# One fused attention and ELU kernel: engine orders written out in a table, one pool of PSUM banks, and batch 0 loaded another way

## The chip, the cores and the metric

The kernel runs on one core of a Trainium2 chip. The metric is the device time of one execution in microseconds. A core has five engines with queues of their own: TensorE (PE; its weight loads are listed as PEld), VectorE (DVE), ScalarE (ACT), GpSimd (POOL) and SyncE (SP, which here only starts transfers). Each works through its own list of instructions in order and waits on semaphores for the others.

## What is computed

Attention over 8 batches and 8 heads, 576 tokens, head size 64, with 16 beacon keys and values ahead of the causal ones, and then an MLP with an ELU on the 4608 rows that come out, 512 -> 2048 -> 512.

```
k_all = concat(beacon_k, k); v_all = concat(beacon_v, v)
scores = q @ k_all.T / sqrt(D)           # causal over k, beacons always seen
a = softmax(scores)
x = (a @ v_all) as rows of 4608 x 512    # (b, s) x (h, d)
h = x @ w_in
out = where(h > 0, h, exp(min(h, 0)) - 1) @ w_out
```

Inputs and output are float32 in HBM.

## The kernel before

**Attention.** Two heads make a pair (n = 0 to 31, four to a batch). For batches 0 to 2, keys and queries of a pair are loaded together into one staging tile (`load_pair`, L308), cast to bf16 (`cast_pair`, L317) and transposed on TensorE (`do_T2`, L394, for batch 0; `do_T`, L384, for 1 and 2); DVE and ScalarE copy the result to `kT` and `qT`. For batches 3 to 7 rows of tokens are loaded (`load_tok`, L332), cast, and transposed by a DMA (`turn_tok`, L350). Scores come out transposed, keys on partitions: `do_SC` (L432) makes four units of a pair, of up to 512 columns for each head, on 64 rows of the array for each head. `do_exp` (L445) takes exp on ScalarE, `do_mask` (L452) clears what is not causal on GpSimd, `do_AV` (L460) multiplies by the values with a column of ones, and `do_norm` (L481) divides by the sums on DVE. Batches 0 and 1 go back through TensorE (`do_xT`, `do_xcopy`) to `xT`, later ones by a DMA (`turn_x`, L357).

**Values.** `load_v` (L362) loads 128 tokens of all heads at a time, each row of a head 256 bytes, from SP or ScalarE's queue; `cast_v` (L371) casts on DVE.

**MLP.** The rows are cut into eleven tiles, 128, 128, 256 and then 512 rows. For each tile sixteen steps (fewer for the small ones) of `do_mm1` (L521) write one bank; `do_e` (exp, ScalarE), `do_clamp` (GpSimd) and `do_join` (DVE) make the ELU; `do_mm2` (L556) sums quarters of the second product, `do_osb` copies it out and `do_store` stores it from SP's queue. Weights come in eight loads from GpSimd's queue, cast on the way (`load_w`, L375).

**What sets the order.** Everything is an `Op` of a `Plan` (L18 to L140) with an engine, a key (its due time), a cost, its dependences, and the buffers that it takes and gives. `Plan.run` plays this through on the host when the kernel is built and writes down each engine's order; the constants from L577 on (SHIFT, AT, PACES, TOK ...) set the keys. Where TensorE would be idle before a planned 30 us it puts in a matmul that computes nothing (`do_fill`, L271).

**PSUM.** Of eight banks, two buffers of two banks have the tag `sc` (scores, and transposes of batches 1 and 2), four of one bank the tag `ff` (the rest). Scores of units (0,1) and (2,3) of a pair are issued together (batch 0: unit 0, units 1 and 2, unit 3).

Of the kernel before, what the change touches and what calls it, by code (L numbers as in the profile page):

```python
# [10 lines left out]
FP32 = mybir.dt.float32  # L11
# [4 lines left out]
P = 128  # L16


class Op:
    def __init__(self, eng, key, dur, fn, deps=(), take=(), give=(), mode=None, lat=0.03, queue=0, parts=1):  # L20
        self.eng, self.key, self.dur, self.fn = eng, key, dur, fn
        self.deps, self.take, self.give = [d for d in deps if d is not None], take, give
        self.mode, self.lat, self.queue, self.parts = mode, lat, queue, parts
        self.left, self.after, self.rest = 0, [], parts


class Plan:
    MODE_COST = 0.1

    def __init__(self, slots, window):  # L30
        self.slots, self.window, self.ops = dict(slots), window, []

    def add(self, *args, **kw):
        op = Op(*args, **kw)
        self.ops.append(op)
        return op

    def run(self):
        for i, op in enumerate(self.ops):
            op.seq = i  # L40
            op.left = len(op.deps)
            for d in op.deps:
                d.after.append(op)
        ready = {op.eng: [] for op in self.ops}
        pending = {eng: sorted((o.key, o.seq) for o in self.ops if o.eng == eng) for eng in ready}
        done = set()
        first = dict.fromkeys(pending, 0)
        free = dict.fromkeys(pending, 0.0)
        mode, lines, turn = None, ([], [], []), 0

        def arrive(o):
            if o.eng == "DMA":
                lines[o.queue].append(o)
            else:
                heapq.heappush(ready[o.eng], (o.key, o.seq))

        for op in self.ops:
            if not op.left:
                arrive(op)
        events, order, now, n_left, tick = [], [], 0.0, len(self.ops), 0  # L60
        while n_left:
            for eng in ready:
                if free[eng] > now + 1e-9:
                    continue
                if eng == "DMA":
                    if any(lines):
                        turn = next((turn + i) % 3 for i in (1, 2, 3) if lines[(turn + i) % 3])
                        op = lines[turn][0]
                        free[eng] = now + op.dur / op.parts
                        heapq.heappush(events, (free[eng], tick, None))  # L70
                        tick += 1
                        op.rest -= 1
                        if not op.rest:
                            lines[turn].pop(0)
                            heapq.heappush(events, (free[eng] + op.lat, tick, op))
                            tick += 1
                    continue
                line = pending[eng]
                while first[eng] < len(line) and line[first[eng]][1] in done:
                    first[eng] += 1  # L80
                if first[eng] == len(line):
                    continue
                limit = line[first[eng]][0] + self.window.get(eng, 1e9)
                skipped, op = [], None
                while ready[eng]:
                    item = heapq.heappop(ready[eng])
                    o = self.ops[item[1]]
                    if item[0] > limit:
                        skipped.append(item)
                        break  # L90
                    if all(self.slots[t] >= o.take.count(t) for t in o.take):
                        op = o
                        break
                    skipped.append(item)
                for item in skipped:
                    heapq.heappush(ready[eng], item)
                if op is None:
                    if eng == "PE" and now < self.fill_until and self.slots["ff"]:
                        mode = 0
                        order.append((now, len(order), self.filler))  # L100
                        free[eng] = now + (self.cold_dur if now < self.cold_until else self.filler.dur)
                        heapq.heappush(events, (free[eng], tick, None))
                        tick += 2
                    continue
                for t in op.take:
                    self.slots[t] -= 1
                start = now
                if op.mode is not None:
                    if mode not in (None, op.mode):
                        start += self.MODE_COST  # L110
                    mode = op.mode
                done.add(op.seq)
                order.append((start, len(order), op))
                free[eng] = start + op.dur
                heapq.heappush(events, (free[eng], tick, None))
                heapq.heappush(events, (free[eng] + op.lat, tick + 1, op))
                tick += 2
            assert events, (self.slots, [(o.key, o.eng, o.left) for o in self.ops if o.seq not in done][:10])
            now = events[0][0]
            while events and events[0][0] <= now + 1e-9:  # L120
                _, _, op = heapq.heappop(events)
                if op is None:
                    continue
                n_left -= 1
                for t in op.give:
                    self.slots[t] += 1
                for o in op.after:
                    o.left -= 1
                    if not o.left:
                        arrive(o)  # L130
        self.length = now
        self.order = order
        for _, _, op in order:
            if op.fn is not None:
                op.fn()
# [3 lines left out]
def kernel(  # L139
# [30 lines left out]

    HALF = P // 2
    G = S // HALF
    assert G * HALF == S
    NKC = -(-SK // P)
# [8 lines left out]
    class Cut:  # L183
        def __init__(self, ranges, splits):
            self.ranges, self.parts, self.units, self.of_range = ranges, [], [], []
            for (lo, hi), split in zip(ranges, splits):
                part = [(jc, max(lo, first_q[jc]), hi - max(lo, first_q[jc])) for jc in range(NKC) if first_q[jc] < hi]
                self.parts.append(part)
                self.of_range.append(list(range(len(self.units), len(self.units) + len(split))))
                for chunks in split:  # L190
                    self.units.append([p for p in part if p[0] in chunks])
            self.col_of, self.width, self.unit_of = {}, [], {}
            for u, unit in enumerate(self.units):
                col = 0
                for jc, q0, w in unit:
                    self.col_of[jc, q0], self.unit_of[jc, q0] = col, u
                    col += w
                assert col <= 512
                self.width.append(col)

    CUT = Cut([(0, 240), (240, 496), (496, 576)], [[(0, 1)], [(0, 1), (2, 3)], [(0, 1, 2, 3, 4)]])

# [5 lines left out]
    def blocks_of(groups):  # L208
        lo, hi = CUT.ranges[groups[0]][0], CUT.ranges[groups[-1]][1]
        return [i for i, (q0, w, _) in enumerate(BLOCKS) if lo <= q0 < hi]  # L210
# [15 lines left out]
    NG, NET, NKQ = 18, 8, 2 * HP  # L226
    NST, NSB, NVST = 6, 3, 6
    PE_B = 3
    konst = ctx.enter_context(tc.tile_pool(name="konst", bufs=1))
    big = ctx.enter_context(tc.tile_pool(name="big", bufs=1))  # L230
    stage = ctx.enter_context(tc.tile_pool(name="stage", bufs=2))
    attn = ctx.enter_context(tc.tile_pool(name="attn", bufs=2))
    melt = ctx.enter_context(tc.tile_pool(name="melt", bufs=4))
    gpool = ctx.enter_context(tc.tile_pool(name="gpool", bufs=NG))
    opool = ctx.enter_context(tc.tile_pool(name="opool", bufs=3))

    ctx.enter_context(tc.manual_schedule())

    identb = konst.tile([P, P], BF16, name="identb")
    make_identity(nc, identb)  # L240
    identh = konst.tile([P, P], FP16, name="identh")
    make_identity(nc, identh)
    fill0 = nc.gpsimd.to_reg(0.0)

    RING = 4 * S
    xTa = big.tile([P, NCC, RING], FP16, name="xT")
    xT = [xTa[:, cc] for cc in range(NCC)]
    w_in16 = big.tile([P, NCC, DF], FP16, name="w_in16")
    w_out16 = big.tile([P, NFC, DM], FP16, name="w_out16")
# [12 lines left out]
    with tc.tile_pool(name="psum", bufs=1, space=bass.MemoryType.PSUM) as psum:  # L262
# [21 lines left out]
        def load(key, dur, fn, deps=(), take=(), issue=0.47, units=1, on="SP"):  # L284
# [3 lines left out]
            if "vst" not in take and on + str(key) != "ACT-899":  # L288
                issues["st"].append(issue)
# [588 lines left out]
```

## Time and profile before

| | us |
|---|---|
| listed runs | 355.49, 1955.26, 353.3 |
| median | 355.49 |
| span of the profiled execution, first to last instruction | 352.5 |
| TensorE busy | 343.3 |
| DVE / ScalarE / GpSimd busy | 205.8 / 194.1 / 179.4 |

The time of the profiled execution itself is not listed; the lowest listed run is 0.8 us above its span. TensorE had its full clock in all slices of the profile. A row of a timeline is start, length, engine, line, operation, what is written <- what is read, and the number of instructions merged; a bracket tells how long the engine was idle before and what ended that. Names such as L473 are lines of the kernel before.

### The profile page before, as it was taken

Reading aid. Unit: us, or ns where it says so; the run is one execution under the profiler, and the core shown is the slowest. Engines: PE = TensorE matmul, PEld = TensorE weight load, DVE = VectorE, ACT = ScalarE, POOL = GpSimd, SP = SyncE. Lnnn points to the kernel's source line nnn. Section 1 sums busy time; section 2 is a strip of 40 time slices with the busy share of each in tenths; the row PEclk is TensorE's granted clock in tenths of the full one; section 3 lists DMA queues with packets and bytes.
Section 4 is the critical chain, followed back from the end, with each engine's and each line's share of the span. In section 5 each row is a group of like instructions: output and inputs, shape, how many; then the busy total and the mean of one; then the engine's idle time right before and its main releaser. Section 6 shows DMA issues by size and latency. Waiting matters only on the chain.

```text
span 352.5 us, 8440 instructions
## 1 busy us (share of the span) xinstructions
PE 343.3 (97%) x3295; PEld 195.6 (55%) x3295; DVE 205.8 (58%) x428; ACT 194.1 (55%) x289; POOL 179.4 (51%) x353
## 2 busy tenths in 40 slices
PE   8999999999999989999999999999999999999996
PEld 5668887545555445545476664554445544444444
DVE  1478797557556567557746565764665555455322
ACT  2586887577556746684576547663477443343200
POOL 5587776556635655475475455463554333434200
PEclk9999999999999999999999999999999999999999
DMA  7999996798998979899999679767460220000112
GB/s 189 260 286 221 206 238 130 227 215 146 165 209 144 208 153 185 160 195 204 152 232 150 146 138 237 143 104 182 96 144 32 60 69 32 31 31 32 47 72 91
DMA packets 139480, 52.55 MB, mean 149 GB/s; under 512 B 127536, under 2 KB 131888, under 8 KB 139440
## 3 DMA queue, kind: packets, MB, share of 16 engines
q1 hardware_dynamic: 87472, 35.55, 46.7%
q10 hardware_dynamic: 47744, 12.26, 18.9%
q0 software_dynamic: 4224, 4.19, 7.1%
q8 instruction: 26, 0.43, 0.5%
q14 instruction: 14, 0.11, 0.1%
HBM read 37.22 MB, written 9.44 MB: 132 GB/s over the span
## 4 chain that ended last, share of the span: by engine, by line
PE 82%; DMA 7%; DVE 4%; SPq 2%; POOL 1%; issue 1%; ACT 1%; ACTq 0%; POOLq 0%; DVEq 0%
PE ops L563 32%; PE hps L529 32%; PE av L473 8%; PE sc L439 7%; DMA st<-in_k_dram 3%; PE spare L274 3%; DMA st<-in_q_dram 2%; DMA xT<-x 1%; SPq L314 1%; DMA kT<-st 1%; DVE gt L549 1%; POOL et L454 1%; DVE x L489 1%; ACT et L448 1%; POOL e L540 1%
## 5 line engine op out<-in xcount | busy, mean ns | idle before, releaser
L529 PE MATMUL hps<-xT,w_in 128*128 128x512 f16 (+2 forms) x768 | 141.4, 326 | 2.8 <-DVE gt L549 1.3
L563 PE MATMUL ops<-w_out,gt 128*128 128x512 f16 (+1 forms) x592 | 143.9, 374 | 0.0
L549 DVE SCALAR_TENSOR_TENSOR gt<-e,hps 128x512 f16<-128x512 f32 x144 | 97.6, 684 | 74.9 <-POOL e L540 74.5
L540 POOL TENSOR_SCALAR e<-e 128x512 f32<-128x512 f32 x144 | 88.1, 614 | 102.4 <-ACT e L536 100.5
L536 ACT ACTIVATE e<-hps 128x512 f32<-128x512 f32 x144 | 85.6, 600 | 94.3 <-PE hps L529 90.2
L448 ACT ACTIVATE et<-sc 128x768 f16<-128x768 f32 (+3 forms) x128 | 104.1, 863 | 31.8 <-PE sc L439 31.6
L529 PEld LDWEIGHTS <-w_in 128*128 128x128 f16 x768 | 68.0, 98 | 57.6 <-issue 3.6
L563 PEld LDWEIGHTS <-gt 128*128 128x128 f16 x592 | 54.1, 98 | 56.5 <-issue 3.0
L454 POOL TENSOR_SCALAR_AFFINE_SELECT et<-et 128x256 f16<-128x256 f16 (+2 forms) x160 | 61.5, 410 | 44.9 <-ACT et L448 40.8
L473 PEld LDWEIGHTS <-et 128*128 128x128 f16 (+1 forms) x960 | 36.1, 97 | 11.0 <-issue 2.2
L569 DVE COPY osb<-ops 128x512 f32<-128x512 f32 (+1 forms) x37 | 25.0, 675 | 26.2 <-PE ops L563 25.3
L473 PE MATMUL av<-v,et 128*128 128x65 f16 (+1 forms) x960 | 39.7, 193 | 0.3 <-DVE x L489 0.3
L439 PE MATMUL sc<-qT,kT 64*128 64x80 bf16 (+3 forms) x704 | 35.2, 228 | 0.3 <-ACT qT L428 0.2
L489 DVE TENSOR_TENSOR x<-av,rl 128x256 f16<-128x256 f32 (+2 forms) x68 | 32.1, 472 | 2.3
L439 PEld LDWEIGHTS <-kT 64*128 64x128 bf16 x704 | 20.7, 95 | 18.9 <-issue 16.8
L488 DVE RECIPROCAL rl<-av 128x4 f32<-128x4 f32 (+2 forms) x68 | 12.4, 182 | 21.4 <-PE av L473 20.3
L373 DVE CAST v<-vst 128x512 f16<-128x512 f32 (+1 forms) x40 | 21.1, 529 | 4.1 <-DMA vst<-in_v_dram 4.1
L274 PE MATMUL spare<-ones 128*128 128x256 bf16 x111 | 19.1, 304 | 1.6 <-DVE ones L816 1.3
L274 PEld LDWEIGHTS <-ones 128*128 128x128 bf16 x111 | 10.9, 109 | 6.2 <-issue 1.7
L346 DVE CAST st<-st 128x1024 bf16<-128x1024 f32 (+2 forms) x18 | 11.6, 655 | 2.8 <-DMA st<-in_k_dram 1.4
L323 POOL CAST st<-st 128x1152 bf16<-128x1152 f32 x8 | 9.1, 1142 | 5.7 <-DMA st<-in_q_dram 3.9
L346 POOL CAST st<-st 128x1024 bf16<-128x1024 f32 (+2 forms) x12 | 10.7, 892 | 2.0 <-DMA st<-in_k_dram 2.0
(35 smaller groups left out, 68.0 us busy)
## 6 DMA issues: line engine op xcount, KB each, us to landing
out_dram<-osb SPq DMA_DIRECT2D x35, 256.0 KB, 2.6
st<-in_q_dram ACTq DMA_DIRECT2D x20, 256.0 KB, 4.3
vst<-in_v_dram ACTq DMA_DIRECT2D x15, 256.0 KB, 4.1
st<-in_k_dram SPq DMA_DIRECT2D x15, 256.0 KB, 5.0
st<-in_k_dram SPq DMA_DIRECT2D x12, 288.0 KB, 7.1
st<-in_q_dram SPq DMA_DIRECT2D x11, 288.0 KB, 6.9
vst<-in_v_dram SPq DMA_DIRECT2D x9, 256.0 KB, 7.0
w_in<-in_moe_w_in_dram POOLq DMA_DIRECT2D x4, 512.0 KB, 12.7
```

The source lines that it names most:

```text
L274: nc.tensor.matmul(out=spare[:, 0:2 * P], lhsT=ones[:, 0:P], rhs=ones, start=True, stop=True)
L439: nc.tensor.matmul(out=sc[:, h, o:o + w], lhsT=kT[D * h:D * h + D, P * jc:P * jc + P], rhs=qT[D * h:D * h + D, q0:q0 + w], start=True, sto ...
L448: nc.scalar.activation(out=et[:, :, 0:w], in_=scs[n, u][:, :, 0:w], func=AFT.Exp, bias=0.0, scale=float(1.0 / (D ** 0.5)))
L454: nc.gpsimd.affine_select(out=et[:, :, c0:c0 + dw], in_=et[:, :, c0:c0 + dw], compare_op=ALU.is_ge, fill=fill0, base=q0 + NB - P * jc, pat ...
L473: nc.tensor.matmul(out=av[:, c:c + D + 1], lhsT=ets[n, CUT.unit_of[jc, at]][0:m, h, col:col + P], rhs=v16[0:m, jc, 2 * hp + h, 0:D + 1], s ...
L489: nc.vector.tensor_tensor(out=x16s[b % 2][:, blks[0]:blks[0] + nb, P * hp:P * hp + P].rearrange("q i (h d) -> q i h d", d=D), in0=av[:, :, ...
L529: nc.tensor.matmul(out=hps[:, o:o + z - a], lhsT=w_in16[:, cc, P * fc:P * fc + P], rhs=xT[cc][:, a % RING:a % RING + z - a], start=(cc == ...
L536: nc.scalar.activation(out=e, in_=hpss[tt, i], func=AFT.Exp, bias=0.0, scale=1.0)
L540: nc.gpsimd.tensor_scalar(out=e, in0=e, scalar1=1.0, scalar2=0.0, op0=ALU.min, op1=ALU.max)
L549: nc.vector.scalar_tensor_tensor(out=gt, in0=es[tt, i], scalar=1.0, in1=hpss[tt, i], op0=ALU.subtract, op1=ALU.max)
L563: nc.tensor.matmul(out=opss[tt, t4][:, cols], lhsT=gts[tt, fc][:, P * t4:P * (t4 + 1)], rhs=w_out16[:, fc, cols], start=(fc == 0), stop=(f ...
L569: nc.vector.tensor_copy(out=osb[:, slice(*cols)], in_=opss[tt, t4][:, slice(*cols)])
```

## The change

The planner is gone. The kernel lists its ops with dependences, buffers and the engines that could do each, and three tables say the rest: ORDER, the order of all ops (with -1 for a filler matmul and the bank that it writes), PICKS, which engine does an op that more than one could do (casts, copies, and SP or ScalarE for starting a load), and PLACES, which buffer each op takes. `Program.run` only plays the tables.

```diff
-        self.slots, self.window, self.ops = dict(slots), window, []
...
+    def run(self, order, picks, places, fill):
+        picks, places, used = iter(picks), iter(places), set()
+        for op in self.ops:
+            if len(op.engines) > 1:
+                op.eng = next(picks)
+        for i in order:
+            if i < 0:
+                at = int(next(places), 36)
+                fill(self.rooms["bank"][at])
+                continue
+            op = self.ops[i]
...
+            for room in op.take:
+                at = int(next(places), 36)
+                held = [("bank", at), ("bank", at + 1)] if room == "pair" else [(room, at)]
...
+                op.fn(self.engines[op.eng], *got, *op.args)
```

PSUM is eight banks in one pool. Scores and the transposes of batches 1 and 2 take an even bank and the next, all else takes one bank; every score unit is now an op of its own.

```diff
-            "sc": 2, "ff": 4, "av": 2, "ops": 1, "et": NET, "rl": 2, "e": NE, "gt": NG, "osb": 3,
...
+    pairs = [psum.tile([P, 2, 512], FP32, name=f"banks_{i}") for i in range(4)]
...
+        "bank": [pairs[i // 2][:, i % 2] for i in range(8)],
+        "pair": [pairs[i // 2] for i in range(8)],
+        "acc": [None, None],
```

Keys and queries of batch 0 are loaded, cast, transposed and copied in two parts, 256 tokens and 320, with a bank for each; scores of unit 0 need only the first part.

```diff
+    CUTS = (0, 256, S)
...
+    def do_T2(e, bank, n, half):
+        tr = trs[n, half] = bank.bitcast(BF16)
...
+        for g in range(g1):
+            e.transpose(
+                out=tr[:, P * g:P * g + P], in_=b16s[n][:, g0 + g].rearrange("p h d -> p (h d)"), identity=identb)
...
+            need = ready if b else ready[0] + (ready[1] if u else [])
```

Of batch 0's values the first 512 of 592 rows (beacons included) are loaded by three DMAs from GpSimd's queue, four tokens to a partition (runs of 1 KB of a head), cast to fp16 on the way, into the room of the last quarter of `w_out16`. TensorE puts them in order: for each 128 rows four matmuls of 32 rows and 512 columns with a matrix of ones and zeros (`sel`, which GpSimd makes by a memset and four selects). ScalarE or DVE copies them out. The last 80 rows, and batches 1 to 7, go the old way. The last quarter of `w_out` is loaded after that.

```diff
+    def do_sel(e):
+        e.memset(sel, 0.0)
+        for c in range(P // 32):
+            e.affine_select(
+                out=sel, in_=sel, compare_op=ALU.not_equal, fill=1.0, base=P * c,
+                pattern=[[-1, VG], [1, P]], channel_multiplier=-VG)
...
+    def load_vq(e, b, part):
+        r0, r1 = [(0, NB // VG), (NB // VG, 64), (64, P)][part]
+        src = beacon_v[b] if part == 0 else v[b, :, VG * r0 - NB:VG * r1 - NB, :]
+        e.dma_start(out=vq[r0:r1], in_=src.rearrange("h (p g) d -> p h (g d)", g=VG))
...
+    def do_P(e, bank0, bank1, b, half):
+        for g in range(VG):
+            for c, bank in ((2 * half, bank0), (2 * half + 1, bank1)):
+                vps[b, c] = bank
+                rows = slice(32 * c, 32 * c + 32)
+                e.matmul(
+                    out=bank, lhsT=sel[rows, g, :], rhs=vq[rows, :, D * g:D * g + D],
+                    start=(g == 0), stop=(g == VG - 1), skip_group_check=True)
```

The memsets of the beacon tiles and of the ends of the exp tiles move from GpSimd to DVE, casts of values and of rows of tokens may be GpSimd's or DVE's for each op, and copies DVE's or ScalarE's. Tiles, matmul shapes, exps, masks and the MLP's steps are as before, and so is what goes through DMA transposes. Counted in the orders that the two programs issue:

| | before | after |
|---|---|---|
| filler matmuls | 111 | 57 |
| matmuls that put values in order | 0 | 16 |
| runs of score matmuls on TensorE, all / behind the first MLP matmul | 68 / 56 | 59 / 48 |
| DMAs started by SP / ScalarE / GpSimd | 191 / 56 / 8 | 181 / 69 / 11 |

On TensorE the changed order starts with 21 fillers, the first half of pair 1, 10 fillers, the first half of pair 2, scores of pair 1, then values in order. Ahead of the first MLP matmul stand all scores, value matmuls and transposes back of batch 0 and the transposes of pairs 6 and 4; before, two of the value matmul ops and four of the transposes back stood behind it. The last stores are issued as the first half of the last block, the whole block before it, the second half.

More of the change, by code (lines that the diff above doesn't have):

```diff
@@ L1 @@
-import heapq
-from functools import partial
 from contextlib import ExitStack
@@ L16 @@
 P = 128
-class Op:
[L20 to L30, printed above, removed]
-        self.slots, self.window, self.ops = dict(slots), window, []
[L33 to L55, printed above, removed]
-        for op in self.ops:
[L58 to L133, printed above, removed]
-            if op.fn is not None:
-                op.fn()
@@ L173 @@
     assert G * HALF == S
+    CUTS = (0, 256, S)
+    GS = [(z - a) // HALF for a, z in zip(CUTS, CUTS[1:])]
+    VG = 4
     NKC = -(-SK // P)
@@ L208, in blocks_of @@
     def blocks_of(groups):
[L209 removed]
+        lo, hi = RANGES[groups[0]][0], RANGES[groups[-1]][1]
         return [i for i, (q0, w, _) in enumerate(BLOCKS) if lo <= q0 < hi]
@@ new lines, with copy, fill @@
+    plan = Program({"P": nc.tensor, "V": nc.vector, "A": nc.scalar, "G": nc.gpsimd, "S": nc.sync, "-": None}, rooms)
+    add = plan.add
+    f32s, b16s, vsts, bks = {}, {}, {}, {}
+    trs, scs, ets, avs, xts, vps = {}, {}, {}, {}, {}, {}
+    hpss, es, gts, opss, osbs = {}, {}, {}, {}, {}
+    def copy(e, out, in_):
+        if e is nc.scalar:
+            e.activation(out=out, in_=in_, func=AFT.Copy)
+        else:
+            e.tensor_copy(out=out, in_=in_)
+    def fill(bank):
+        nc.tensor.matmul(out=bank[:, 0:2 * P], lhsT=ones[:, 0:P], rhs=ones, start=True, stop=True)
@@ new lines, in cast_pair, with cast_pair2, do_T @@
+    def cast_pair(e, sb, n, half):
+        b16s[n] = sb
+        cast_pair2(e, n, half)
+    def cast_pair2(e, n, half):
+        if half is None:
+            dst, src, g = b16s[n], f32s[n], G
+        else:
+            g = GS[half]
+            g0 = CUTS[half] // HALF
+            dst, src = b16s[n][:, g0:g0 + g], part_of(f32s[n], half)
+        copy(e, dst.rearrange("p g h d -> p h g d"), src.rearrange("p h (g d) -> p h g d", g=g))
+    def do_T(e, pair, n):
+        b, hp = divmod(n, HP)
+        tr = trs[n] = pair.rearrange("p a b -> p (a b)").bitcast(BF16)
+        for g in range(G):
+            e.transpose(out=tr[:, P * g:P * g + P], in_=b16s[n][:, g].rearrange("p h d -> p (h d)"), identity=identb)
+        e.transpose(out=tr[:, P * G:P * G + P], in_=bk16s[b % 2][:, P * hp:P * hp + P], identity=identb)
@@ new lines, in turn_x, with do_xT @@
+    def turn_x(e, b, blk):
+        q0, rows, _ = BLOCKS[blk]
+        e.dma_start_transpose(
+            out=xTa[:, :, b * S % RING + q0:b * S % RING + q0 + rows], in_=x16s[b % 2][0:rows, blk, :])
+    def do_xT(e, bank, n, groups):
+        b, hp = divmod(n, HP)
+        xt = xts[n, groups[0]] = bank.bitcast(FP16)
+        lo = RANGES[groups[0]][0]
+        for blk in blocks_of(groups):
+            q0, rows, _ = BLOCKS[blk]
+            e.transpose(
+                out=xt[:, q0 - lo:q0 - lo + rows], in_=x16s[b % 2][0:rows, blk, P * hp:P * hp + P],
+                identity=identh[0:rows, 0:rows])
@@ new lines, in add_tok @@
+    def add_tok(b):
+        turned[b] = []
+        for is_k in (True, False):
+            for c in range(0, NKC, 2):
+                m = min(2, NKC - c)
+                st = add("SA", load_tok, b, is_k, c, take=["st"])
+                got = [st] + ([add("SA", load_tok2, b, is_k, c + 1, deps=[st])] if m == 2 else [])
+                cast = add("GV", cast_tok, b, is_k, c, m, deps=got, take=["sb"], give=[(st, 0)])
+                for j in range(m):
+                    before = [o for hp in range(HP) for o in last_SC.get((b - 2) * HP + hp, [])]
+                    turned[b].append(add("S", turn_tok, b, is_k, c + j, deps=[cast] + before))
+                add("-", None, deps=turned[b][-m:], give=[(cast, 0)])
@@ new lines @@
+    gts_in = {}
+    make_identity(nc, identb)
+    make_identity(nc, identh)
+    nc.vector.memset(ones, 1.0)
+    for t in kTa:
+        nc.vector.memset(t[:, :, SK:SKP], 0.0)
+    for t in bk16s:
+        nc.vector.memset(t, 0.0)
+    for et in rooms["et"]:
+        nc.vector.memset(et[:, :, WIDTH[-1]:WIDTH[-1] + P - BLOCKS[-1][1]], 0.0)
+    for t in v16s:
+        nc.vector.memset(t[:, :, :, D:VW], 1.0)
+    sel_done = add("G", do_sel)
+    for b in range(B):
+        add_batch(b)
+    for f4 in range(4):
+        add_w(0, f4)
+        add_w(1, f4)
@@ L851 @@
+    for p in range(NTT):
+        add_tile(p)
+    for b, t in turns:
+        t.deps += readers.get(b - RING // S, [])
+    plan.run(ORDER, PICKS, PLACES, fill)
 _INS = ['q', 'k', 'v', 'beacon_k', 'beacon_v', 'moe_w_in', 'moe_w_out']
```

955 lines of the change are left out of this document (409 added, 546 removed), and 71 rows, old and new, of the table ORDER.

## The prediction

> **What bounds the kernel now.** I read the page first, then the stage table, then the timelines of TensorE, ScalarE and GpSimd over the first 36 us, the groups by form, the DMA view of two stretches, and the waits.
>
> ```profile
> span 352.5 us, 8440 instructions
> PE 343.3 (97%) x3295; PEld 195.6 (55%) x3295; DVE 205.8 (58%) x428; ACT 194.1 (55%) x289; POOL 179.4 (51%) x353
> ...
> PE 82%; DMA 7%; DVE 4%; SPq 2%; POOL 1%; issue 1%; ACT 1%; ACTq 0%; POOLq 0%; DVEq 0%
> ```
>
> TensorE is busy for 97% of the span and holds 82% of the chain that ended last. A sum over the run hides stages, so the stage table is cut at the first matmul of the MLP (31.9 us), and at the last matmul. Its columns are the stretch, its length, then busy time and count of each engine, the granted clock, the DMA share and GB/s.
>
> ```profile
> 0.00:31.90 31.90, 28.91 (x364) 20.91 (x365) 16.36 (x54) 17.58 (x26) 22.10 (x50) 1.00 1.08 238
> 31.90:60.00 28.10, 27.82 (x458) 23.44 (x458) 22.95 (x54) 22.34 (x35) 19.72 (x38) 1.00 1.10 210
> 60.00:150.00 90.00, 88.06 (x897) 46.94 (x896) 55.25 (x118) 55.51 (x80) 47.85 (x97) 1.00 0.93 178
> 150.00:349.40 199.40, 198.51 (x1582) 104.35 (x1582) 110.82 (x204) 98.64 (x150) 89.69 (x171) 1.00 0.54 114
> 349.40:352.60 3.20, 0.00 (x0) 0.00 (x0) 0.41 (x1) 0.00 (x0) 0.00 (x0) 1.00 0.27 99
> ```
>
> From 31.9 to 349.4 us TensorE is idle for 0.28 + 1.94 + 0.89 = 3.1 us. No order of the engines can win more than that there, except by making TensorE's own work shorter. The first stretch is different. The same view for the filler matmuls alone:
>
> ```profile
> 0.00:31.90 31.90, 19.05 (x111) 10.86 (x111) 1.00 1.08 238
> ```
>
> 111 of the 364 matmuls there compute nothing; they stand where TensorE would wait. So the gain to look for is in the first 32 us, a smaller one in TensorE's own work, and the 3.2 us of the last store stay.
>
> **The start.** The MLP's first matmul needs all four head pairs of batch 0 through exp, so ScalarE's queue sets the time. Rows of the timelines, one of the stage table, then of the groups by form (count | busy us, mean ns):
>
> ```profile
> 1.83 0.98 POOL L820 MEMSET bk<- 128x512 bf16 x2
> ```
> ```profile
> 5.80 1.14 POOL L323 CAST st<-st 128x1152 bf16<-128x1152 f32 x1 [2.03 <-DMA st<-in_q_dram]
> ```
> ```profile
> 9.76 0.78 ACT L448 ACTIVATE et<-sc 128x736 f16<-128x736 f32 x1 [1.17 <-PE sc L439]
> ```
> ```profile
> 9.76:31.90 22.14, 20.55 (x311) 15.21 (x310) 14.70 (x46) 15.52 (x23) 16.97 (x30) 1.00 1.20 256
> ```
> ```profile
> L448 ACT ACTIVATE et<-sc 128x768 f16<-128x768 f32 (+3 forms) x128 | 104.1, 863 | 31.8 <-PE sc L439 31.6
> ```
> ```profile
> L536 ACT ACTIVATE e<-hps 128x512 f32<-128x512 f32 x144 | 85.6, 600 | 94.3 <-PE hps L529 90.2 <-DVE x L489 1.8 <-DVE st L346 1.2
> ...
> L454 POOL TENSOR_SCALAR_AFFINE_SELECT et<-et 128x256 f16<-128x256 f16 x96 | 39.6, 428 | 21.3 <-ACT et L448 20.0 <-PE hps L529 0.5
> ...
> L373 DVE CAST v<-vst 128x512 f16<-128x512 f32 x32 | 17.3, 540 | 4.1 <-DMA vst<-in_v_dram 4.1
> ...
> L454 POOL TENSOR_SCALAR_AFFINE_SELECT et<-et 128x160 f16<-128x160 f16 x32 | 11.6, 364 | 0.7 <-ACT et L448 0.6
> ...
> L428 ACT ACTIVATE qT<-tr 128x576 bf16<-128x576 bf16 x8 | 5.2, 649 | 5.9 <-DVE kT L423 4.7 <-PE av L473 1.2
> ...
> L380 POOL DMA_DIRECT2D w_out<-in_moe_w_out_dram x4 | 3.7, 920 | 0.0
> ```
>
> First exp. Batch 0's keys and queries now come as two loads each, the first 256 of 576 tokens. The old first cast began at 5.80 when 288 KB of queries landed; 128 KB should land between a proportional 3 us and 5.8, I take 5.5. The cast is now DVE's (540 ns for 512 elements), so pair 1 is transposed at 6.1. Its first scores stand behind pair 2's transposes on TensorE, whose cast is on GpSimd behind two value loads (920 ns each), a memset of 512 elements (0.5 us, as each of the two at 1.83) and four selects of 512 elements. From 428 ns at 256 and 364 ns at 160 elements a select grows by 0.67 ns per element, so 0.6 us each. The other memsets leave GpSimd for DVE, which is idle then. GpSimd: 1.8 + 1.8 + 0.5 + 2.4 = 6.5, plus a cast of 0.6 (half of the 1.14): 7.1; half a pair's transposes, scores and handovers, about 1.1 us: first exp at 8.2 instead of 9.76.
>
> ScalarE's queue from there to the last exp of batch 0: 16 exps at 104.1 / 128 = 0.81 (13.0), two copies of ordered values like the 600 ns ACTIVATE (1.2), two query copies of at most 649 ns (1.3): 15.5 us. If ScalarE never waited it would end at 23.7. Before, from 9.76 to 31.9, ScalarE (the fourth engine of the row) was busy 15.5 of 22.1 us, so it waited 6.6. Waits of 0 to 6.6 us give 23.7 to 30.3. I take 3, near the middle: transfers still come late, but each half needs only half of them. Then 26.7; plus the last values matmuls, reciprocal and multiply, transpose and copy, about 1.5 us: first MLP matmul at 28.2 (25.2 to 31.8) instead of 31.9. **Term 1: -3.7 us** (-6.7 to -0.1).
>
> In the changed order every value matmul and transpose back of batch 0 and two transposes of batch 1 stand ahead of that matmul. Before, two sets of ten value matmuls, five transposes back and the ten transposes of a pair of batch 1 stood behind it; that matmul's row and their rates, by starts:
>
> ```profile
> 31.91 1.05 PE L529 MATMUL hps<-xT,w_in 128*128 128x128 f16 x16 [0.54 <-DVE xT L510]
> 32.80 0.28 PE L499 MATMUL xt<-identh,x 128*128 128x128 f16 x2
> 32.91 0.47 PE L473 MATMUL av<-v,et 128*128 128x65 f16 x10
> 33.23 0.20 PE L499 MATMUL xt<-identh,x 80*128 80x80 f16 x1
> ```
>
> Ten value matmuls take 0.32 us (32.91 to 33.23), two transposes 0.11 (32.80 to 32.91). So 0.64 + 15 x 0.055 = 1.5. **Term 2: -1.5 us.** The 16 matmuls that put the values in order (512 columns, at most 0.22 us each by the rows below: 1.8 to 3.5 us) come before it too, in place of 54 fillers that are gone (57 are left), so nothing for them, unless ScalarE waits for their copies; that is in the 0 to 6.6.
>
> **TensorE's own work.** Scores run on 64 rows of the array, all else on 128. The switch shows in the starts:
>
> ```profile
> 139.57 0.52 PE L439 MATMUL sc<-qT,kT 64*128 64x256 bf16 x14
> 140.02 0.35 PE L473 MATMUL av<-v,et 128*128 128x65 f16 x6
> 140.21 1.89 PE L563 MATMUL ops<-w_out,gt 128*128 128x512 f16 x8
> 142.03 0.55 PE L439 MATMUL sc<-qT,kT 64*128 64x240 bf16 x8
> 142.52 1.90 PE L563 MATMUL ops<-w_out,gt 128*128 128x512 f16 x8
> 144.26 0.35 PE L473 MATMUL av<-v,et 128*128 128x65 f16 x6
> ```
>
> Eight matmuls take 1.74 us before values (142.52 to 144.26) and 1.82 before scores (140.21 to 142.03): 0.08 to enter. Units 2 and 3 are 784 columns, with both heads side by side 0.33 us at 512 columns in 0.218, and take 0.45 (139.57 to 140.02): 0.12 to leave. Behind the first MLP matmul the old order enters scores 56 times, the new one, which places single units and groups those of several pairs, 48 times: 8 x 0.2. **Term 3: -1.6 us.** [...]
>
> **Waits behind.** The eight banks in one pool and finer score units could remove the 3.1 us of idle time; a fixed order over five queues could add as well. I take no change: -3 to +14 (rival C). **Tail:** the second-last store is now issued right before the last and shares the engines with it: +0.2 (0 to +1, by the 3.2 us row). DVE's memsets at the start (2 us) stand before its first cast and cost nothing while data are on the way.
>
> Sum: -3.7 - 1.5 - 1.6 + 0.2 = -6.6: span 345.9. The lowest run shown, 353.3, is 0.8 over the profiled span; with that the time is **346.7**. The median shown, 355.5, is 2.2 above its own execution; against it this is -2.5%, against 353.3 -1.9%. A difference under about 2% can't be told from none here.
>
> **Rivals.** *A, better:* ScalarE never waits in the start and half of the later idle time goes: -3.0 - 1.6, time 342.1. For it: it waited 6.6 us there, and most of its idle rows end with TensorE, which had fillers in hand; against: the DMA engines are full throughout that stretch (share 1.08).
>
> *B, no gain in the start, since transfers set it.* DMA queue rows (packets, MB, share of 16 engines) of 0 to 34 us and of 300 to 345 us, where only stores run:
>
> ```profile
> q10 hardware_dynamic: 4976, 1.51, 22.6%
> ```
> ```profile
> q1 hardware_dynamic: 1032, 1.88, 11.2%
> ```
>
> In the first, 0.226 x 16 x 34 = 123 us for 4976 packets: 25 ns for 303 B, 12 B/ns. In the second, 0.112 x 16 x 45 = 81 us for 1032 packets: 78 ns for 1822 B, 23 B/ns. Values of batch 0 went in rows of 256 B, now 88% of them go in runs of 1 KB, so they cost the engines about half: 1.05 MB at 12 B/ns on 16 engines is 5.5 us, at 23 B/ns 2.9. That speaks for the change. Against it: two of their three loads now run ahead of or beside the first keys, on a third queue. [...] No row here shows GpSimd's queue in the first 20 us. As a mechanism of this kernel: 1.05 MB at the 238 GB/s of the first stretch is 4.4 us; if all of that stands in front of the keys of pairs 2, 0 and 3, it eats the 3.7 of term 1: time 350.4.
>
> *C, slower: ScalarE held at its own DMA issues.* By the order that the two programs issue, ScalarE issues 69 DMAs instead of 56, SP 181 instead of 191, GpSimd 11 instead of 8 (the three value loads). [...]
>
> ```profile
> ACT e L536 <- DVE x L489: 1.8, 1, 1.8
> ```
> ```profile
> SPq L369 <- DVE rl L488: 6.2, 2, 5.7
> ```
>
> Before, such a wait held ScalarE for 1.8 us once; on SP, where nothing else stands behind, one for a value load took 5.7. When ScalarE stops, TensorE goes on until its banks are full: eight banks are at most eight MLP steps, 4 x 0.218 each, 7 us, but four score units or fewer when scores are next, about 1 us. Three waits of 5.7 us that meet a run of scores, less 1 us each, are 14.1 us: 346.7 + 14.1 = 360.8. It decides from 6.6 us of uncovered waits on, which is the whole sum.
>
> **Chances.** Forecast 0.46 (own range 343.5 to 349.5), A 0.13, B 0.21, C 0.20. Against the median shown, 2% less is 348.4, against the lowest run 346.2. So faster by over 2% takes A and four fifths of the forecast: 0.13 + 0.37 = 0.50. Within 2%: the rest of the forecast and B, 0.09 + 0.21 = 0.30. Slower by over 2%: C, 0.20. The range goes from A to B with the 3 to 5 us of the waits' bounds on top: 341.5 to 356.0; C and a little below A stay out.
>
> **What would show it.** Term 1: the first MLP matmul at 25.2 to 31.8, 57 fillers, the first exp near 8.2 and ScalarE's waits from there to its last exp of batch 0. Term 2: no transpose back of batch 0 behind that matmul. Term 3: 48 entries into scores, with the same 0.2 for each. Waits: TensorE's idle time from there to the last matmul near 3 us; over 10 with ScalarE behind a DMA issue is C. B: value matmuls or pair 0's cast waiting for their loads past 11 us. It would be wrong if TensorE's idle time grew with no DMA behind it, for instance where a bank that the table names is freed late while another is free, or if the first MLP matmul came no earlier than 31.

## The result, and the profile after

The changed kernel takes 477.62 us in the median (477.41 to 480.24, 5 runs) where the kernel before takes 353.67: ratio 1.348 (95% interval 1.340 to 1.356), 35% slower. The forecast was 346.7, its range ended at 356.0. The profiled execution took 480.24 us, its span is 478.2. Lines of the kernel after are named as in its profile. Its page:

```profile
span 478.2 us, 8360 instructions
...
PE 371.6 (78%) x3257; PEld 205.6 (43%) x3257; DVE 203.5 (43%) x429; ACT 193.6 (40%) x290; POOL 180.7 (38%) x363
...
PE 57%; DVE 13%; ACT 9%; DMA 7%; issue 5%; POOL 5%; SPq 3%; DVEq 0%; ACTq 0%; POOLq 0%
...
L550 PE MATMUL banks<-xT,w_in 128*128 128x512 f16 (+2 forms) x768 | 148.2, 345 | 45.4 <-DVE gt L568 25.5
L588 PE MATMUL banks<-w_out,gt 128*128 128x512 f16 (+1 forms) x592 | 142.3, 384 | 28.7 <-DVE gt L568 12.0
```

TensorE fell from 97% to 78% of the span, and no other engine took over: each is below half. The last two rows are the two products of the MLP. Together they stood idle 74 us, and what ended the idle time is ahead of all DVE's join, an engine that is busy 43% of the time. The stage table, cut again at the first MLP matmul and the last matmul; the first fence is before in one stretch, the second after:

```profile
31.91:349.40 317.49, 314.40 (x2931) 174.73 (x2930) 189.01 (x375) 176.48 (x264) 157.25 (x304) 1.00 0.70 141
```
```profile
0.00:43.37 43.37, 30.19 (x361) 21.30 (x362) 21.09 (x75) 18.37 (x27) 22.34 (x48) 0.83 0.97 222
43.37:473.60 430.23, 341.44 (x2897) 184.28 (x2896) 181.69 (x353) 175.25 (x264) 158.31 (x315) 0.94 0.48 97
473.60:478.20 4.60, 0.00 (x0) 0.00 (x0) 0.73 (x2) 0.00 (x0) 0.00 (x0) 0.71 0.33 114
```

From these rows the 125.7 us between the two spans (478.2 less 352.5) come apart: the start +11.5 (43.37 less 31.91), TensorE's idle time behind it +85.7 (430.23 - 341.44 = 88.8, less 3.1), its busy time there +27.0, and the tail +1.4 (4.6 less 3.2). So most of it is waiting, spread over the whole run, with a lower granted clock on top. The waits, summed over the span (times, longest):

```profile
ACT e L557 <- DVE gt L568: 26.1, 18, 3.4
PE banks L550 <- DVE gt L568: 25.5, 14, 5.1
DVE gt L568 <- PE banks L550: 22.4, 7, 7.7
DVE gt L568 <- PE banks L588: 20.4, 10, 3.7
PE banks L550 <- ACT e L557: 12.4, 12, 2.9
PE banks L588 <- DVE gt L568: 12.0, 9, 2.2
PE banks L588 <- ACT e L557: 8.7, 8, 2.2
```

Some of these make no sense by the algorithm. A join (L568) needs the first product and the clamped exp, not a result of the second product (L588). In the profile of before, no join of DVE waited for a matmul of the second product and no MLP matmul of TensorE for an exp of ScalarE. One such wait in the timeline:

```profile
227.54 0.62 ACT L557 ACTIVATE e<-banks 128x512 f32<-128x512 f32 x1
...
228.21 1.89 PE L550 MATMUL banks<-xT,w_in 128*128 128x512 f16 x8 [2.86 <-ACT e L557]
```

By the PLACES table this matmul writes bank 3, and the exp that it waited 2.86 us for reads bank 2. Nothing else joins the two: banks 2 and 3 are the two halves of one declared tile, `pairs[1]`.

### The profile page after: what moved, and what is told of

Same layout as the page of the kernel before. It is cut to its first block, busy times and chain, and to the rows that moved or that the text cites. A ratio compares the mean times of both kernels' runs of the same rounds, so it can differ in the third digit from the quotient of the medians.

```text
span 478.2 us, 8360 instructions
## 1 busy us (share of the span) xinstructions
PE 371.6 (78%) x3257; PEld 205.6 (43%) x3257; DVE 203.5 (43%) x429; ACT 193.6 (40%) x290; POOL 180.7 (38%) x363
## 4 chain that ended last, share of the span: by engine, by line
PE 57%; DVE 13%; ACT 9%; DMA 7%; issue 5%; POOL 5%; SPq 3%; DVEq 0%; ACTq 0%; POOLq 0%
PE banks L588 25%; PE banks L550 22%; DVE gt L568 6%; ACT e L557 6%; PE banks L498 6%; POOL e L561 4%; DMA st<-in_q_dram 3%; DVE x L512 2%; DMA vst<-in_v_dram 2%; PE banks L468 2%; ACT et L477 2%; DMA st<-in_k_dram 2%; DVE osb L594 2%; PE banks L349 1%; DVE rl L511 1%
## 5 line engine op out<-in xcount | busy, mean ns | idle before, releaser
L550 PE MATMUL banks<-xT,w_in 128*128 128x512 f16 (+2 forms) x768 | 148.2, 345 | 45.4 <-DVE gt L568 25.5
L588 PE MATMUL banks<-w_out,gt 128*128 128x512 f16 (+1 forms) x592 | 142.3, 384 | 28.7 <-DVE gt L568 12.0
L568 DVE SCALAR_TENSOR_TENSOR gt<-e,banks 128x512 f16<-128x512 f32 x144 | 94.7, 684 | 135.0 <-POOL e L561 71.7
L557 ACT ACTIVATE e<-banks 128x512 f32<-128x512 f32 x144 | 82.6, 598 | 148.4 <-PE banks L550 93.8
L477 ACT ACTIVATE et<-banks 128x1024 f16<-128x1024 f32 (+3 forms) x128 | 104.6, 863 | 91.8 <-PE banks L468 81.2
L588 PEld LDWEIGHTS <-gt 128*128 128x128 f16 x592 | 56.7, 99 | 92.4 <-issue 39.6
L498 PE MATMUL banks<-v,et 128*128 128x65 f16 (+1 forms) x960 | 42.5, 199 | 12.6 <-ACT e L557 3.4
L594 DVE COPY osb<-banks 128x512 f32<-128x512 f32 (+1 forms) x37 | 24.8, 674 | 48.5 <-PE banks L588 37.2
L468 PE MATMUL banks<-qT,kT 64*128 64x80 bf16 (+3 forms) x704 | 36.1, 234 | 7.9 <-DVE gt L568 3.4
L512 DVE TENSOR_TENSOR x<-banks,rl 128x256 f16<-128x256 f32 (+2 forms) x68 | 32.1, 471 | 2.3
L404 DVE CAST sb<-st 128x1024 bf16<-128x1024 f32 (+2 forms) x21 | 12.6, 610 | 0.0
L294 POOL CAST sb<-st 128x512 bf16<-128x512 f32 (+2 forms) x7 | 5.5, 796 | 11.5 <-DMA st<-in_q_dram 11.3
```

What stands on the lines that cost most here:

```text
L294: e.tensor_copy(out=out, in_=in_)
L468: e.matmul(out=pair[:, h, o:o + w], lhsT=kT[D * h:D * h + D, P * jc:P * jc + P], rhs=qT[D * h:D * h + D, q0:q0 + w], start=True, stop=True ...
L477: e.activation(out=et[:, :, 0:w], in_=scs[n, u][:, :, 0:w], func=AFT.Exp, bias=0.0, scale=float(1.0 / (D ** 0.5)))
L498: e.matmul(out=av[:, c:c + D + 1], lhsT=ets[n, unit_of[jc, at]][0:m, h, col:col + P], rhs=v16s[b % 2][0:m, jc, 2 * hp + h, 0:D + 1], start ...
L512: e.tensor_tensor(out=x16s[b % 2][:, blks[0]:blks[0] + nb, P * hp:P * hp + P].rearrange("q i (h d) -> q i h d", d=D), in0=av[:, :, :, 0:D] ...
L550: e.matmul(out=bank[:, o:o + z - a], lhsT=w_in16[:, cc, P * fc:P * fc + P], rhs=xTa[:, cc, a % RING:a % RING + z - a], start=(cc == 0), st ...
```

## The theory, and the experiments

**Theory S (shared tiles).** The eight banks are declared as four tiles of two banks. By this theory the framework that sets the semaphores orders a write of a tile behind every open use of that tile, and a read behind its last write, whichever half they touch. So two ops in neighbouring banks wait for each other. In the built program of after, some 130 of TensorE's instructions and some dozens each of DVE's and ScalarE's wait for one that touched only the neighbour bank. In that of before hardly any do: there only scores and the transposes of batches 1 and 2 had tiles of two banks, and a unit or pair used both. **Rival O (order).** The written-out order, or which bank the table names, sets the waits; tiles don't matter.

**One bank per tile.** So that each instruction stays within a tile, each exp of scores is cut in two, one per head, and the copies out of the transposes of batches 1 and 2 too. Order, picks and places are as they were.

```diff
-    pairs = [psum.tile([P, 2, 512], FP32, name=f"banks_{i}") for i in range(4)]
+    banks = [psum.tile([P, 512], FP32, name=f"banks_{i}") for i in range(8)]
...
-        e.activation(
-            out=et[:, :, 0:w], in_=scs[n, u][:, :, 0:w], func=AFT.Exp, bias=0.0, scale=float(1.0 / (D ** 0.5)))
+        for h in range(2):
+            e.activation(
+                out=et[:, h, 0:w], in_=scs[n, u][h][:, 0:w], func=AFT.Exp, bias=0.0, scale=float(1.0 / (D ** 0.5)))
```

> The changed kernel with its eight PSUM banks as eight tiles of one bank instead of four tiles of two. For that an exp of scores becomes two (one per head and bank), and the two copies out of a transposed pair of batches 1 and 2 become two each; order, engines and places are the same. Theory S (shared tiles): in the changed kernel a wait covers the whole tile of two banks, so an MLP matmul waits for exp and join of the neighbour bank, and DVE and ScalarE wait for TensorE writing the neighbour. Then these waits go: no MLP matmul waits for an exp of the MLP any more (12.4 us in the changed kernel), TensorE's idle time falls by over 80 of its 107 us, time 350 to 380 (128 more exps at some 0.2 us each land on ScalarE, which is idle for 60% of the span). Rival O (fixed order): the written order itself does not fit the real durations, so each engine waits in its own queue whatever the tiles are: still over 440 us.

Measured: 359.12 us (before 354.47; ratio 1.014, 1.007 to 1.021). The same two groups and the stage row of this run:

```profile
L555 PE MATMUL banks<-xT,w_in 128*128 128x512 f16 (+2 forms) x768 | 135.2, 326 | 0.8 <-DVE gt L573 0.4
L593 PE MATMUL banks<-w_out,gt 128*128 128x512 f16 (+1 forms) x592 | 136.0, 374 | 0.7 <-DMA w_out<-in_moe_w_out_dram 0.7
```
```profile
29.44:352.90 323.46, 314.87 (x2899) 174.47 (x2897) 184.02 (x368) 181.07 (x379) 159.81 (x315) 1.00 0.71 139
```

Their idle time went from 74.1 us to 1.5, with the same order. The exps of one head took 532 ns on average where those of both took 863, so two are 0.20 us longer than one, as expected; but ScalarE was busy only 6.2 us longer over the run (199.8 against 193.6), since they overlap (256 of 532 ns are 136 us, busy for 112.3). The control has the same cuts, but keeps four tiles of two banks:

> The control for the run with eight tiles: the same doubled exps and copies, but the banks stay four tiles of two. Theory S: nothing gets better, 475 to 505 us, the upper end if ScalarE's 25 us more land on the path. Rival (the gain of the other run comes from handing over one head's exps earlier, not from the tiles): 350 to 440 us.

Measured: 485.4 us (one run). The cuts win nothing; the tiles do.

**The same fault put into the kernel before.** Its four one-bank buffers of tag `ff` are taken from two tiles of two banks, handed out oldest first; in the control from four tiles of one bank, handed out in the same way.

```diff
+        ffs = [psum.tile([P, 2, 512], FP32, name=f"ffs_{i}") for i in range(2)]
+        room = [ffs[i // 2][:, i % 2] for i in range(4)]
...
-        room = [ffs[i // 2][:, i % 2] for i in range(4)]
+        room = [psum.tile([P, 512], FP32, name=f"ffs_{i}") for i in range(4)]
```

> The converse in the kernel before: its four single banks are taken from two tiles of two banks, oldest freed bank first; planner and order of every engine as before. Theory S: the MLP steps of a tile's two banks wait for each other; a step is 0.87 us of matmuls, then exp 0.60, clamp 0.62 and join 0.68 with handovers, some 3 us on a tile, two tiles, so 16 steps of a row tile take some 24 us instead of 14, part of it covered by the second product: over 390 us. Rival O: sharing a tile does not matter, 350 to 362 us.

> The control for the converse: the kernel before with its four single banks as four tiles that are kept for the whole run, oldest freed bank first, so it differs from the last one in the tiles alone. Both theories: as the kernel before, 350 to 362 us. If it is slower than that, the way in which banks are handed out costs by itself, and the converse says that much less on the tiles.

Measured: 420.62 and 351.94 us (one run each). The planner's order, with not one op moved, loses 68.7 us when its banks share tiles, and shows the same senseless rows:

```profile
PE ffs L545 <- ACT e L552: 4.1, 6, 1.4
...
DVE gt L565 <- PE ffs L580: 21.2, 15, 3.4
```

Rival O is out as the cause of this loss; what the order still costs without shared tiles comes below.

**The changed kernel, with the needless waits alone taken out.** Each pair of instructions on different engines that touch different banks of a tile, and share nothing else, is declared independent; no instruction is moved or cut.

```diff
+                for old, h, shared in seen:
+                    if not h & halves and old.engine != ins.engine and not shared & others:
+                        self.tc.declare_no_dep(ins, old, reason="the other bank")
```

> The changed kernel as it is, with the same instructions, order, engines, places and tiles of two banks, but for each two instructions on different engines that touch different banks of one tile (and share no other buffer) the program is told that neither waits for the other. Theory S: TensorE's idle time behind the first MLP matmul is below 10 us, first MLP matmul at 28 to 30 us; the run with eight tiles took 359.1 with 5.7 us more busy time on ScalarE and 8.6 us of idle TensorE between 40 and 350 us, so this one takes 345 to 357, on either side of the kernel before (354). If the prediction was right but for the shared tiles, 347. Rival O: the doubled exps of the run with eight tiles also helped by handing scores over in halves; then 365 or more.

Measured: 358.09 us (357.07 to 360.83; ratio 1.011, 1.006 to 1.016). So these waits cost 119.5 us of the 477.6. But the time stays a little above the range that S had given, and above before. The stages, and one row of the start:

```profile
30.96:351.10 320.14, 313.53 (x2897) 174.55 (x2896) 182.44 (x353) 173.50 (x264) 160.01 (x315) 1.00 0.71 140
351.10:355.70 4.60, 0.00 (x0) 0.00 (x0) 0.71 (x2) 0.00 (x0) 0.00 (x0) 0.92 0.32 114
```
```profile
30.27 0.63 ACT L322 ACTIVATE xT<-banks 128x240 f16<-128x240 f16 x2 [2.69 <-DVE xT L324]
```

The same 2897 matmuls are busy 313.5 us here and 341.4 in after, at granted clocks of 1.00 and 0.94. In the last row ScalarE waits 2.69 us for DVE's write of other columns of `xT`: the same fault in SBUF, new with copies back that are dealt to two engines.

The waits between banks are needless by the data flow; whether they guard anything else no trace here shows. The 358.09 us show what they cost.

**What else separates it from before.** The next four steps start from the run without the bank waits and build on one another, but for the third, which is undone again. Each moves the median by some 1 us or less, no more than the runs of one kernel scatter (352.82 to 357.23 for the kernel before, 29 runs), so what a step did is read from the rows of its profile more than from its median. First, the same for other elements of the tiles of `xT`, `kT`, `qT` and the values, between the compute engines:

> As the run in which other banks of a tile no longer wait for each other (358.1), and the same for other elements of the transposed tiles: x, keys, queries, values and the normalised rows, between the compute engines. In that run ScalarE's copy back of pair 3 to the tile of x waited 2.7 us for DVE's copies of other rows and pairs into that tile, and the first MLP matmul waited 1.4 us for ScalarE's copy. Theory S (a wait covers a tile, and the table gives writes of one tile to two engines): the first MLP matmul comes at 28.0 to 29.5 instead of 30.96, time 355.0 to 357.5. Rival: ScalarE has other work in hand there, so nothing changes: 30.5 to 31, 358.

Measured: 356.98 us (ratio 1.005, 1.002 to 1.008), as expected. Second, the last matmuls and copies in the order of before: first half of the last block, the block before it, second half. For that the last block's first matmul no longer stands behind that block. After issues its last stores in the same order, but does the matmuls of the two blocks one after the other:

```diff
-1763 1764 1760 1761 1765 1766 1768 1769 1772 1773 1770 1774 1771 1767 1775
+1768 1769 1760 1761 1770 1771 1762
+1763 1764 1765 1766 1767 1772 1773 1774 1775
```

> The run before this one, and at the end the order of the kernel before: the first half of the last block's second product, then the whole block ahead of it, then the second half, each copied and stored when it is done. In the changed order DVE's copy of the first half stands behind the matmuls of the second half in the same bank, and both halves are copied in one go at 351.06. Theory: 1.0 to 1.6 us less than the run before this one. Rival (the end is set by the last store alone): within 0.4 us.

Measured: 356.40 us. The tail shrank from 4.6 to 3.5 us, 1.1 as expected; the median only by 0.6, less than expected. The last copies with the old tail (in the run with only the bank waits gone), then with the new one:

```profile
351.06 0.75 DVE L624 COPY osb<-banks 128x256 f32<-128x256 f32 x2 [2.80 <-PE banks L618]
```
```profile
351.41 0.42 DVE L644 COPY osb<-banks 128x256 f32<-128x256 f32 x1 [1.05 <-PE banks L638]
```

In after's order the first half's copy stands behind the second half's matmuls in the same bank, so both copies and both stores come at the end.

Third, what rival C had named: six loads (keys and queries of pairs 8 and 10, two row blocks of batch 3's keys; ops 298 to 416) come sooner in SP's order, five of them taken from ScalarE's queue. Three of these start over 20 us sooner, by SP at 35 to 37 us where ScalarE had started them at 57 to 58 (both of pair 8, the keys of pair 10). The row blocks stand behind a load that SP starts at 60 us itself; one of them, at 59 us before, gains nothing.

> As the last one, with six loads moved: keys and queries of pairs 8 and 10, and rows of batch 3's keys, are started by SP right behind the loads of pairs 9 and 11 (some 36 us) instead of by ScalarE behind the last exps of batch 1 (59 to 62 us); their staging buffers were free from 22.6, 27.2 and 38.6 us. Theory: the DMA engines, used for 0.7 of the time from 40 to 60 us, are filled there, the waits of scores for transposed queries at 105 us (1.8 us) and of transposes at 65 to 70 us shrink, 1 to 4 us less: 350 to 354.5, on a par with the kernel before or better. Rival: these transfers were not what was waited for, within 0.7 us of the last run.

Measured: 357.41 us, a miss: no gain, and 1.0 us more than the run before it. ScalarE's wait of 4.3 us behind a key load was gone and nothing got faster, so the issues of these loads are not what holds the rest. TensorE's wait for DMA transposes of batch 3's queries grew from 1.8 to 3.2 us:

```profile
PE banks L518 <- DMA qT<-sb: 3.2, 1, 3.2
```

Fourth, against that wait, with the loads of the third undone: four loads sooner (431 and 432 behind 437, 176 behind 178, 981 behind 979; the first three on SP).

> The run with the tail in the old order (356.4), and four loads started sooner, each one that TensorE waited behind in it: the second pair of row blocks of batch 3's queries from SP at some 77 us instead of from ScalarE at 87 and 90 (scores waited 1.9 us for the transposed queries at 102 us), one block of batch 1's values from SP at 30 us instead of from ScalarE at 40 (value matmuls waited 0.8 us at 51.6), and the last quarter of the second weight at 44 us instead of 55 (the second product waited 1.1 us at 60.7). Theory L (in the waits that are left each load is late by itself): up to 3.8 us less, 352.6 to 355. Rival T (whoever is early waits for the next late transfer, as when six other loads were moved): 355.5 to 357.5.

Measured: 357.15 us: its rival. The rows land in time, but their casts stand late in DVE's order, and the transposes behind them:

```profile
95.46 0.89 DVE L454 CAST sb<-st 128x1024 bf16<-128x1024 f32 x1
...
96.38 3.44 SPq L459 DMA_TRANSPOSE qT<-sb  x2
...
103.66 0.77 PE L518 MATMUL banks<-qT,kT 64*128 64x256 bf16 x12 [2.54 <-DMA qT<-sb]
```

So with two of those casts (of batch 3's queries) and their transposes sooner too (438 behind 430, 433 behind 1121; 439, 434 and 435 behind 423):

> The run with four loads started sooner (357.2), and two casts of batch 3's queries moved ahead on DVE, with their three DMA transposes on SP: in that run the rows had landed by some 78 us, but DVE's order has the casts behind joins of the MLP at 92.2 and 95.5 us, and scores waited 2.5 us at 101 us for the transposes behind them. Theory F (the written order, not the transfer, is what is late there): the 2.5 us go, 1.5 to 3 us less, and with the gap the spells of half clock behind it, 352 to 355.5. Rival: the waits move on to the next late place, 356 to 358.

Measured: 352.98 us against 354.55 before (351.17 to 356.6; ratio 0.996, 0.994 to 0.999). This is far below after, and 0.4% (0.1 to 0.6) below before, a small lead. The median fell by 4.2 us where a wait of 2.5 was taken away. Its stages:

```profile
0.00:27.88 27.88, 24.56 (x360) 17.34 (x361) 18.95 (x71) 17.99 (x26) 22.16 (x48) 1.00 1.02 229
27.88:346.50 318.62, 313.89 (x2899) 174.35 (x2897) 183.47 (x359) 173.87 (x264) 160.97 (x315) 1.00 0.73 142
346.50:350.00 3.50, 0.00 (x0) 0.00 (x0) 0.40 (x1) 0.00 (x0) 0.00 (x0) 0.88 0.25 90
```

## Why the prediction was wrong

**The step that failed** is "Waits behind: the eight banks in one pool [...] could remove the 3.1 us of idle time; a fixed order over five queues could add as well. I take no change: -3 to +14". TensorE's idle time there became 88.8 us. The step took each of eight banks as a resource of its own, and looked for delays in the order and in DMA queues. The line `pairs = [psum.tile([P, 2, 512] ...) for i in range(4)]` is quoted in the diff; what it does to the semaphores wasn't asked. The prediction's last sentence came near ("a bank that the table names is freed late while another is free") but meant the table's choice; it was a free bank that waited for its neighbour's reader. The step also had no term for what gaps do to TensorE's own rate: +27.0 us of busy time.

**Term 1, the start,** forecast -3.7 us, first MLP matmul at 28.2: 43.37 in after, 30.96 without the waits between banks, 29.08, 28.14, 27.54 and 27.88 in the four profiles that are free of those in SBUF as well (the one with the moved loads left aside). The size was right, its parts only in sum. In the second of these, by ScalarE's timeline, the first exp came at 9.15 instead of 8.2, and the last exp of batch 0 ended at 25.98 instead of 26.7: it waited some 1.4 us in between (16.8 less 15.4 of work), not 3. The late first exp is rival B in small: GpSimd's cast of pair 2 waited for its load; what held that load back isn't shown. In the run with only the bank waits gone:

```profile
8.59 0.61 POOL L324 CAST sb<-st 128x512 bf16<-128x512 f32 x1 [1.85 <-DMA st<-in_q_dram]
```

**Terms 2 and 3, TensorE's work behind the start,** -1.5 and -1.6: added up from start to start in the traces, gaps left out, that work is 2.2 to 2.6 us less in the run with only the bank waits gone, by how the gaps are taken off. Of it, 1.6 is in value matmuls and transposes (term 2), 0.6 to 1.0 in the rest, mostly scores (term 3, too large by 0.6 to 1.0). The busy times of the stage rows, whose ends are modelled, show 0.9 of it (314.40 and 313.53).

**The tail,** +0.2 (0 to +1): +1.4, outside its bounds. I had counted 0.2 for two stores at once, and they show it: the two of 128 KB in after's tail landed 1.9 us after their issue (median), the one of before after 1.7. Both copies at the end, in one bank, was the greater cost: with the two apart the tail is 1.1 us shorter.

**Waits behind, without the tiles:** 6.6 us of idle time instead of 3.1 (320.14 less 313.53), +3.5 and inside -3 to +14. With the last edits it is 4.7. So the forecast's sum of -6.6 became -2.6 in span (349.9 against 352.5) in the best version: -4.0 from the start, +1.1 behind it, where -3.1 had been taken, and +0.3 from the tail.

**Rivals.** A (342.1) never came about: the start was won, the later idle time wasn't. Nor did B as a whole, as the start won 4.0 us without the shared tiles; 512 of 592 rows of values are 86%, not its 88%, which changes nothing in its price. C's place was wrong: ScalarE did wait behind its own loads, but taking the longest such wait (4.3 us) away won nothing. None of the cases held the one that happened.

What stays open: why part of the runs of the last versions but the best take 357 us or more, most of them at mean granted clocks of 0.98 to 0.995, where those of before stay at 0.995 or above. The profile with the new tail, at 0.995, holds one slow spell that cost 1.7 us (last section); whether the longer runs hold more of them no profile shows. Open is too how much of after's waiting each single wait between banks costs, since one delays the next.

## What to carry to other kernels

Look at how a buffer is declared, not only at how it is handed out: where waits are set for whole tiles, two banks of one tile act as one resource for TensorE, DVE and ScalarE alike, here 477.6 us where 358.1 are enough without the waits between banks. Look in a profile for waits that the data flow can't explain (a join behind the second product, 20.4 us here, an MLP matmul behind another step's exp, 12.4 us): here they came from a shared tile; look up which half each side touches. When an order is written out by hand, look at what stands behind a load as well: here, moving loads sooner won nothing until their casts and transposes moved with them.

## What the runs showed of the hardware

In after, gaps cost twice, since the granted clock fell with them (0.94 where it was 1.00 without the bank waits). TensorE between 328 and 352 us:

```profile
328.89 3.63 PE L550 MATMUL banks<-xT,w_in 128*128 128x512 f16 x16
337.66 3.57 PE L550 MATMUL banks<-xT,w_in 128*128 128x512 f16 x8 [5.14 <-DVE gt L568]
343.39 3.57 PE L550 MATMUL banks<-xT,w_in 128*128 128x512 f16 x8 [2.16 <-DVE gt L568]
...
349.00 3.60 PE L550 MATMUL banks<-xT,w_in 128*128 128x512 f16 x8
```
```profile
336.00:352.00 16.00, 11.44 (x48) 4.63 (x48) 2.37 (x4) 2.28 (x4) 3.63 (x7) 0.50 0.20 50
```

Sixteen matmuls took 3.6 us ahead of the gap of 5.14 us; behind it eight take as long, at a granted clock of 0.50 for the whole stretch, with more gaps in it. A slow spell stood behind a shorter gap as well. With the new tail (its page's row of the granted clock first, in 40 slices), then in the best version, the same twelve matmuls of the second product near 103 us:

```profile
PEclk9999999999998999999999999999999999999999
```
```profile
104.35 0.77 PE L518 MATMUL banks<-qT,kT 64*128 64x256 bf16 x12 [1.84 <-DMA qT<-sb]
105.05 4.45 PE L638 MATMUL banks<-w_out,gt 128*128 128x512 f16 x12
```
```profile
102.08 2.76 PE L638 MATMUL banks<-w_out,gt 128*128 128x512 f16 x12
```

Behind a gap of 1.84 us they took 4.45 us, 1.7 more than without one. The granted clock is below 0.9 there in one slice alone, from 106.5 to 115.3 us. Behind the 2.54 us of the run before the last, the first eight of them took 1.90 us, as eight do in the best version at 105.40 us, and the granted clock of its stage row is 1.00:

```profile
27.54:349.10 321.56, 313.57 (x2899) 174.62 (x2897) 183.92 (x358) 173.81 (x264) 161.06 (x315) 1.00 0.72 141
```
```profile
104.37 1.90 PE L638 MATMUL banks<-w_out,gt 128*128 128x512 f16 x8
```

So the length of one gap alone doesn't decide it, and what does isn't shown.
